# Second bias tile made in pieces under the first attention tile and parked in DRAM, with a new lead table for the first MoE

## The chip, the cores and the metric

One core of one Trainium2 chip runs the whole program. The metric is the device time of one execution in microseconds (us). Engines are named as in the profile: PE (TensorE), DVE (VectorE), ACT (ScalarE), POOL (GpSimd), and SP, whose queue issues all DMAs of this kernel.

## The reference, cut to what matters

Attention with a learned bias, then two MoE layers, in float32:

```python
x = (log1p(|i - j|) / log1p(max(i, 1)))[..., None]        # 576 x 576
bias = relu(x @ w1 + b1) @ w2                             # one 576 x 576 matrix for each of 8 heads
scores = q @ k.T / 8 + bias                               # 4 batches, 8 heads, 576 positions, depth 64
attn = softmax(scores); x = attn @ v                      # -> 2304 tokens of 512
x = (silu(x @ w_gate) * (x @ w_val)) @ w_out              # first MoE, hidden 1536
out = relu(x @ w_in) ** 2 @ w_out2                        # second MoE, hidden 2048
```

## The kernel before, in words

The 576 query positions are cut into four tiles of 128 (t = 0, 1, 2, 3) and a rest of 64, which is handled for two heads at once (t = "m"). For each tile `attend` walks over *items*, one item being one batch and one head: 32 items for each of the tiles 0 to 3 and 16 merged ones for the rest, 144 in all. An item is a score product on PE (`scores`, L813, four matmuls; L808 in the rest), the bias added and the row minimum taken on DVE (`soft`, L822), the exponential on ACT, a transpose of the result, and the product with v. In tile 0 the transpose is done on PE (L851) and the product with v is L865. In the later tiles the result is split in two float16 halves on POOL (L834, L220), transposed by a DMA (`pT<-pt`, issued on SP at L859), and multiplied by v in L875. In tile 1 `load_pair` and `split_pair` also fetch v again, split it, and store the split form in DRAM (`v_d`), beside loading k from DRAM (`kp<-kT_d`).

The bias matrix does not depend on the batch. `make_bias(t)` makes it for one tile and all eight heads before that tile's items use it. It works in 18 blocks of 32 key positions. Each block takes one mask on DVE (L605), 16 matmuls of 64 columns on PE (L644) into one PSUM bank, and an evacuation that turns the bank into 32 columns of the bias. The evacuation alternates between two forms: two instructions on DVE (L623, L629), or two on ACT (L620, L626) and two on POOL (L621, L627). The bias of a tile lies in one of two rooms of SBUF, `room0` and `room1`: tile 0 in room 1, tile 1 in room 0, tile 2 in room 1. While tile 0 is computed, room 0 also holds k and v of every second load and the results of tile 0 (`kvb` is room 0).

The first MoE (`moe1`) works in nine *units* of 256 tokens. Each attention tile makes two units ready, the rest makes the ninth. A unit has 288 matmuls for gate and value (L459, 24 for each of twelve blocks, each followed by tanh and products in `th` on ACT and DVE, L467 to L470, and a split in `z`, L444 and L220) and 72 for the output projection (L482). Its weights are decoded from 64-bit floats on DVE (`decode`, L262 to L267) and split by `w_stream`, which runs merged with tile 0.

All of this is written as Python generators that yield an estimated cost. `merge` mixes several of them by rates; `a_all` is the attention stream (tile 0 merged with the weights, then `rest`, which makes bias 1 by itself and then runs tiles 1 to 3 and "m", each merged with the next bias, and last `weights2`, which prepares the second MoE). `m_all` is the stream of the nine units. The outer loop steps the units' stream only when the attention stream is far enough ahead by a table:

```python
lead = base is not None and pos["a"] >= base + float(np.interp(pos["m"], *LEAD))
if m_ok and (lead or not a_ok):
    step("m", sm)
```

`pos` is the yielded cost of each stream, and one unit is 46.8 of it. A scheduler then fixes the order of instructions on each engine from this program order. Each engine and the SP queue work strictly in that order. After tile "m" and `weights2`, the second MoE (L1377, L1409) runs on PE to the end.

## Time and profile before

| | us |
|---|---|
| three runs of the kernel before | 1240.95, 1244.9, 1245.37 |
| their median | 1244.9 |
| the profiled execution's own time | 1241.07 |
| its span, from first to last instruction | 1238.9 |
| PE, DVE, ACT, POOL busy in that span | 1089.9, 778.1, 678.0, 651.8 |

A busy time is the union of the spans of an engine's instructions. A matmul's span is partly modelled and overlaps its neighbour's, so a PE that shows busy all through a stretch need not work at its peak. In the tables by stretch "(x91)" is the number of instructions, the column after the engines is the granted TensorE clock (1.00 is 2.4 GHz, 0.50 is 1.2 GHz, a value between is a mean over the stretch), and the last two are the mean busy share of the 16 DMA engines and what they moved.

### The profile page before, as it was taken

Reading aid. Unit: us, or ns where it says so; the run is one execution under the profiler, and the core shown is the slowest. Engines: PE = TensorE matmul, PEld = TensorE weight load, DVE = VectorE, ACT = ScalarE, POOL = GpSimd, SP = SyncE. Lnnn points to the kernel's source line nnn. Section 1 sums busy time; section 2 is a strip of 40 time slices with the busy share of each in tenths; the row PEclk is TensorE's granted clock in tenths of the full one; section 3 lists DMA queues with packets and bytes.
Section 4 is the critical chain, followed back from the end, with each engine's and each line's share of the span. In section 5 each row is a group of like instructions: output and inputs, shape, how many; then the busy total and the mean of one; then the engine's idle time right before and its main releaser. Section 6 shows DMA issues by size and latency. Waiting matters only on the chain.

```text
span 1238.9 us, 27332 instructions
## 1 busy us (share of the span) xinstructions
PE 1089.9 (88%) x10550; PEld 812.1 (66%) x10550; DVE 778.1 (63%) x1864; ACT 678.0 (55%) x1370; POOL 651.8 (53%) x835
## 2 busy tenths in 40 slices
PE   2577899998678889999997999979789999999998
PEld 2466788686467568686774767556348476584787
DVE  5988957887677667656665745895573442624423
ACT  3567767557566566566663543366462643616433
POOL 2433213269768687878784452237791532705423
PEclk9789799999979999999999999989999999999999
DMA  9957543219999998997989995660010010010100
GB/s 222 263 136 206 179 132 87 50 58 198 222 218 204 227 212 165 231 186 162 191 161 257 248 220 142 206 188 1 17 34 19 18 43 27 20 33 17 27 27 17
DMA packets 278078, 163.20 MB, mean 132 GB/s; under 512 B 233276, under 2 KB 246588, under 8 KB 277948
## 3 DMA queue, kind: packets, MB, share of 16 engines
q1 hardware_dynamic: 277948, 161.46, 55.0%
q8 instruction: 82, 1.34, 0.5%
q14 instruction: 48, 0.39, 0.1%
HBM read 92.13 MB, written 19.48 MB: 90 GB/s over the span
## 4 chain that ended last, share of the span: by engine, by line
PE 45%; DMA 14%; POOL 10%; DVE 8%; issue 5%; ACT 4%; SPq 2%; POOLq 0%; ACTq 0%; DVEq 0%
PE mm L1377 12%; PE mm L459 11%; PE mm L1409 10%; DMA pT<-pt 3%; PE mm L482 3%; POOL pt L220 3%; POOL x L1189 2%; PE ma L1409 2%; PE av L875 2%; PE qk L813 2%; DMA w2s<-in_moe_w_out_dram 2%; DMA qT<-qs 2%; DMA scrap<-in_moe_w_in_dram 1%; DMA kp<-kT_d 1%; DMA xT<-xh 1%
## 5 line engine op out<-in xcount | busy, mean ns | idle before, releaser
L459 PE MATMUL mm<-xT,wr 128*128 128x256 f16 x2400 | 288.7, 276 | 14.9 <-DVE th L470 7.3
L459 PEld LDWEIGHTS <-wr 128*128 128x128 f16 x2592 | 251.6, 99 | 53.2 <-issue 19.3
L1189 POOL TENSOR_TENSOR x<-x 128x256 f32<-128x256 f32 (+1 forms) x160 | 142.7, 903 | 178.1 <-ACT x L1386 171.7
L220 POOL TENSOR_TENSOR pt<-s,pt 128x512 f16<-128x512 f32 x224 | 172.1, 791 | 31.5 <-ACT pt L837 26.7
L220 POOL TENSOR_TENSOR z<-th,z 128x256 f16<-128x256 f32 x108 | 79.8, 740 | 129.5 <-ACT z L444 124.7
L482 PE MATMUL mm<-wr,z 128*128 128x512 f16 x612 | 142.3, 379 | 1.6 <-DVE sc L829 1.3
L822 DVE CUSTOM_DVE_ANT_0 s<-qk,room 128x576 f32<-128x576 f32 x144 | 107.7, 748 | 39.9 <-PE qk L813 22.6
L1409 PEld LDWEIGHTS <-wr 128*128 128x128 f16 x1134 | 110.6, 98 | 22.7 <-DVE wr L1189 4.3
L830 ACT ACTIVATE s<-s,sc 128x576 f32<-128x576 f32 x112 | 85.6, 772 | 56.6 <-DVE sc L829 47.1
L1189 DVE TENSOR_TENSOR wr<-x,wr 128x768 f16<-128x768 f32 (+3 forms) x60 | 75.4, 1268 | 64.5 <-ACT wr L1196 63.3
L1377 PE MATMUL mm<-wr,w2r 128*128 128x512 f16 (+1 forms) x480 | 102.2, 364 | 5.0 <-ACT x L1382 5.0
L482 PEld LDWEIGHTS <-z 128*128 128x128 f16 x648 | 60.0, 98 | 66.4 <-issue 2.8
L605 DVE TENSOR_TENSOR scrap<-scrap,room 128x1024 f16<-128x1024 f16 (+1 forms) x108 | 87.3, 822 | 22.4 <-PE ma L644 19.8
L1377 PE MATMUL mm<-wr,room 128*128 128x512 f16 (+1 forms) x480 | 100.1, 358 | 0.0
L621 POOL TENSOR_TENSOR scrap<-scrap 128x256 f32<-128x256 f32 (+1 forms) x90 | 63.2, 702 | 65.9 <-ACT scrap L620 58.2
L875 PE MATMUL av<-vp,pT 128*128 128x65 f16 (+3 forms) x1792 | 70.4, 196 | 28.3 <-DMA pT<-pt 24.3
L875 PEld LDWEIGHTS <-pT 128*128 128x128 f16 (+1 forms) x1792 | 61.7, 102 | 43.2 <-DMA pT<-pt 32.7
L1377 PEld LDWEIGHTS <-w2r 128*128 128x128 f16 x480 | 47.6, 99 | 52.7 <-issue 8.6
L644 PEld LDWEIGHTS <-scrap 128*128 128x128 f16 x1440 | 59.6, 104 | 27.4 <-issue 11.9
L1377 PEld LDWEIGHTS <-room 128*128 128x128 f16 x480 | 46.9, 98 | 45.6
L1428 ACT ACTIVATE ob<-ob,fac 128x256 f32<-128x256 f32 x36 | 17.8, 506 | 105.5 <-DVE ob L1427 105.5
L444 ACT CAST z<-th 128x256 f16<-128x256 f32 x108 | 42.8, 399 | 59.0 <-DVE th L470 57.8
(289 smaller groups left out, 2157.2 us busy)
## 6 DMA issues: line engine op xcount, KB each, us to landing
kp<-kT_d SPq DMA_DIRECT2D x64, 288.0 KB, 3.5
vp<-v_d SPq DMA_DIRECT2D x48, 325.0 KB, 3.5
w2s<-in_moe_w_out_dram SPq DMA_DIRECT2D x16, 512.0 KB, 4.0
wr<-in_moe_w_gate_dram SPq DMA_DIRECT2D x24, 256.0 KB, 5.2
wst<-in_moe_w_out_dram SPq DMA_DIRECT2D x12, 512.0 KB, 4.0
wr<-in_moe_w_val_dram SPq DMA_DIRECT2D x24, 256.0 KB, 4.2
v_d<-vp SPq DMA_DIRECT2D x16, 325.0 KB, 3.1
y_d<-yh SPq DMA_DIRECT2D x18, 256.0 KB, 3.5
```

Of the source, the lines that this page charges most:

```text
L220: nc.gpsimd.tensor_tensor(out=out_, in0=x, in1=hi, op=ALU.subtract)
L459: nc.tensor.matmul(pg[:, 256 * gi:256 * gi + 256], wr.parts(key, f // 4, cc, wl, P * (f % 4), P), mov(xl, cc), start=k == 0, stop=k == 11)
L482: nc.tensor.matmul(po, zall[:, f, zl, P * t:P * t + P], wr.parts("o", 0, f, wl), start=k == 0, stop=k == 3 * NF1 - 1)
L605: nc.vector.tensor_tensor(out=m[:, :, ni * e:ni * e + ni], in0=block(kb, i0, ni), in1=th, op=ALU.is_gt)
L621: nc.gpsimd.tensor_tensor(out=tmp[r], in0=tmp[r], in1=xb, op=ALU.mult)
L644: nc.tensor.matmul(pv[:, :, :, c:c + 4], m[:, a, :], bd[:, l], start=l == 0, stop=l == 1)
L822: nc.vector.tensor_tensor_reduce(out=s.rearrange("p (a j) -> p a j", a=2), in0=pq[:, :, 0:288], in1=bias[:, n].rearrange("p (a j) -> p a j ...
L830: nc.scalar.activation(s, s, AF.Exp, bias=nm, scale=-1.0)
L875: nc.tensor.matmul(av[r, slot, 0:cn], pT[:, 5 * l + c, r], vs[e][c][:, c0:c0 + cn], start=m == 0, stop=m == 13)
L1189: (nc.gpsimd if how else nc.vector).tensor_tensor(out=out_, in0=a, in1=b, op=op)
L1377: nc.tensor.matmul(ph[:, :n], w2r.parts("w", g // 4, cc, wl, P * (g % 4), P), yt[:, 4 * yl + cc, :], start=m == 0, stop=m == 11)
L1409: nc.tensor.matmul(po, HS[f][:, o:o + P], st["C7"][f][wl][:, b:b + 256], start=f == 0 and k == 0, stop=f == 7 and k == 2)
```

## The change: what it does

`make_bias(1)` no longer stands alone ahead of tile 1. It is a third generator merged with tile 0 and the weight stream. Each of its 18 blocks waits until a given number of tile 0's items are done (`("av", 8 + kb)`), makes its mask only then, takes its PSUM bank from the two `mm` banks that the weight stream and the units use (before: from the score banks), and is evacuated into one of two small buffers (`bst`), from where a DMA stores it in DRAM (`b_d`). At the start of `rest`, `fetch_bias` reads the 18 blocks back into room 0 with three DMAs. The addition in `soft` reads them through a four-dimensional view for tile 1. The lead table gets other numbers: less of the units at first, more from the end of the second unit on.

```diff
-LEAD = [0, 39, 78, 117, 260, 400], [0, 85.669, 132.183, 165.544, 287.094, 406.094]
+LEAD = [0, 28, 93.6, 327, 400], [0, 82.0, 127.0, 333.0, 389.0]
...
+    b_d = dram.tile([P, 18, 256], F32, name="b_d")
...
-        merged = t == "m"
+        merged, afar = t == "m", t == 1
...
-        bias = rooms[{0: 1, 1: 0, 2: 1, 3: 0, "m": 1}[t]]
+        bias = rooms[0 if t == 3 else 1]
...
+                to = bst[:, kb % 2] if afar else bias[r, :, cs]
...
                     nc.vector.scalar_tensor_tensor(
-                        out=bias[r, :, cs], in0=pv[r, 1, hs], scalar=st["kB"][r], in1=tmp[r],
+                        out=to, in0=pv[r, 1, hs], scalar=st["kB"][r], in1=tmp[r],
                         op0=ALU.mult, op1=ALU.add)
+                if afar:
+                    nc.sync.dma_start(b_d[:, kb, :], to.rearrange("p h j -> p (h j)"))
...
-            if kb + 1 < nb:
+            if kb + 1 < nb and not afar:
                 mask(kb + 1)
+            if afar:
+                yield ("av", 8 + kb)
+                mask(kb)
             m = masks.pop(kb)
-            pv = ma().rearrange("p (z h j) -> p z h j", z=2, h=8)
+            pv = (mm if afar else ma)().rearrange("p (z h j) -> p z h j", z=2, h=8)
...
+    def fetch_bias():
+
+        room = rooms[0][:, 0:8 * S].rearrange("p (k x) -> p k x", k=18)
+        for k0, k1 in ((9, 13), (0, 9), (13, 18)):
+            nc.sync.dma_start(room[:, k0:k1], b_d[:, k0:k1])
+        st["bias", 1] = room.rearrange("p k (h j) -> p h k j", h=8)
...
+    bst = pre.tile([P, 2, 8, 32], F32, name="bst")
...
+        fetch_bias()
         scale_v(ma)
-        early[0] = True
-        yield from make_bias(1)
-        early[0] = False
...
-        yield from merge((sa, 25.5), (w_stream(), 70.0))
+        yield from merge((sa, 25.5), (w_stream(), 70.0), (make_bias(1), 30.0))
```

The order of instructions shows it at three places. Line numbers of the changed kernel are higher: L844 there is the softmax addition that is L822 before, L607 the mask L605, L626 and L632 the two DVE evacuations L623 and L629, L666 the fetch.

The first place is DVE in the second half of tile 0, at the additions of the items with index 18 and 19 (`ISA s`). Before, the stretch ahead of an addition holds weight decoding (`wr<-wst`) and splitting:

```order
L265 SCALAR_TENSOR_TENSOR wr_97<-wst_128,wr_97 128x512
L904 TENSOR_REDUCE sc_1615<-sc_1308 128x1
L751 COPY qs_1764<-qs_1764 128x4x64
L267 SCALAR_TENSOR_TENSOR wr_97<-wst_128,wr_97 128x512 x2
L191 SCALAR_TENSOR_TENSOR wr_97<-wr_97,keep11_1255 128x512
L822 ISA s_1698,sc_1699<-qk_1687,room1_115 128x576
L822 ISA sc_1699 128x1
```

With the change:

```order
L844 ISA s_1872,sc_1873<-qk_1777,room1_116 128x576
L844 ISA sc_1873 128x1
L760 SCALAR_TENSOR_TENSOR qs_2007<-qf_2005,qs_2007 128x4x64
L626 SCALAR_TENSOR_TENSOR scrap_117<-mm_1602,keep4_216,scrap_117 128x256
L607 TENSOR_TENSOR scrap_117<-scrap_117,room1_116 128x1024
L192 SCALAR_TENSOR_TENSOR wr_98<-wr_98,keep11_1260 128x512
L844 ISA s_1920,sc_1921<-qk_1886,room1_116 128x576
L844 ISA sc_1921 128x1
```

An evacuation and a mask of bias 1 now stand between two additions of tile 0. In the whole order 12 of the 18 masks stand ahead of tile 0's last addition, 3 of them in its first sixteen items.

The second place is DVE at the first additions of tile 1, which read room 0. Before, masks and evacuations of the biases alternate with the `th` products of the second unit:

```order
L468 SCALAR_TENSOR_TENSOR th_3932<-th_3932,mm_3905 128x256
L629 SCALAR_TENSOR_TENSOR room0_114<-qk0_3185,keep4_214,scrap_116 128x8x32
L605 TENSOR_TENSOR scrap_116<-scrap_116,room1_115 128x1024
L470 SCALAR_TENSOR_TENSOR th_3932<-th_3932,mm_3905 128x256
L822 ISA s_3277,sc_3278<-qk_3244,room0_114 128x576
L822 ISA sc_3278 128x1
```

With the change:

```order
L192 SCALAR_TENSOR_TENSOR vp_3120<-junk1_114,keep25_3106,vp_3120 64x2x64
L469 SCALAR_TENSOR_TENSOR th_3194<-th_3194,mm_3167 128x256
L471 SCALAR_TENSOR_TENSOR th_3194<-th_3194,mm_3167 128x256
L192 SCALAR_TENSOR_TENSOR wr_98<-wr_98,keep23_2661 128x512
L607 TENSOR_TENSOR scrap_117<-scrap_117,room1_116 128x1024
L844 ISA s_3198,sc_3199<-qk_3140,room0_115 128x576
L844 ISA sc_3199 128x1
```

The `th` products here are still those of the first unit. On PE, 336 matmuls of L459, 72 of L482 and 288 of L644 stand between the last score of tile 0 and the first of tile 1 before; with the change 186, none and 112. By the items with index 56 to 64 the two orders have issued the same unit matmuls again to within a few blocks.

The third place is the SP queue ahead of tile 1's first loads of k (`kp`). Before:

```order
L739 DMA qf_3853<-in_q_dram 128x4x64
L765 DMA kp_3222<-kT_d0_63 128x1152
L765 DMA kp_3237<-kT_d0_63 128x1152
L925 DMA_TRANSPOSE xT_2706<-xh_2707 128x8x128
L925 DMA_TRANSPOSE xT_2706<-xh_2711 128x8x128
L776 DMA junk1_113<-in_v_dram 64x2x64
```

With the change:

```order
L600 DMA scrap_117<-in_c_x_dram 128x576
L636 DMA b_d_71<-bst_130 128x256 x2
L946 DMA_TRANSPOSE xT_3076<-xh_3081 128x8x128
L666 DMA room0_115<-b_d_71 128x1280
L781 DMA kp_3118<-kT_d0_63 128x1152
L781 DMA kp_3133<-kT_d0_63 128x1152
```

The two loads of k stood ahead of the second unit's transposes (`xT`); they now stand behind them and behind the last stores and the last fetch of bias 1.

## Rows read from the trace of the kernel before

**Rows 1.** Engine busy time by stage: the eleven stretches of this study, all engines

```profile
core 0: us, PE busy (x) PEld busy (x) DVE busy (x) ACT busy (x) POOL busy (x), PEclk, DMA share, GB/s
67.40:130.60 63.20, 50.02 (x432) 41.39 (x430) 55.43 (x130) 46.04 (x88) 18.68 (x15) 0.94 0.68 173
130.60:197.20 66.60, 57.00 (x484) 50.88 (x482) 46.81 (x134) 51.51 (x111) 14.96 (x13) 0.87 0.48 146
197.20:270.60 73.40, 69.61 (x765) 55.90 (x763) 58.24 (x148) 40.51 (x90) 31.80 (x39) 1.00 0.21 58
270.60:303.40 32.80, 30.23 (x393) 25.01 (x393) 25.47 (x68) 24.65 (x54) 29.84 (x40) 1.00 0.76 164
303.40:361.80 58.40, 42.02 (x481) 28.92 (x480) 40.19 (x109) 34.76 (x78) 44.40 (x63) 0.80 1.00 221
361.80:402.80 41.00, 35.59 (x445) 30.54 (x444) 31.24 (x79) 28.32 (x65) 32.11 (x48) 1.00 0.95 206
402.80:456.50 53.70, 46.16 (x539) 32.40 (x539) 35.31 (x105) 31.48 (x62) 38.66 (x53) 0.97 1.03 222
456.50:519.60 63.10, 63.08 (x766) 49.48 (x765) 42.73 (x127) 38.70 (x81) 52.51 (x73) 1.00 0.93 191
519.60:743.00 223.40, 202.61 (x2492) 154.13 (x2490) 137.72 (x432) 127.01 (x277) 150.46 (x234) 0.98 0.95 206
743.00:930.00 187.00, 162.32 (x1167) 103.36 (x1166) 129.41 (x268) 98.69 (x200) 98.78 (x95) 0.96 0.34 97
930.00:1238.90 308.90, 302.83 (x2206) 215.19 (x2204) 122.84 (x152) 127.61 (x218) 113.20 (x132) 1.00 0.09 25
```

**Rows 2.** Line L813, score matmuls of tiles 1 to 3

```profile
L813 PE MATMUL qk<-kp,qT x384: 282/286/448, 270.6 to 658.4; 128*128 128x288 f16 x192
```

**Rows 3.** Groups of instructions, 235 to 272 us, lines of make_bias

```profile
L605 DVE TENSOR_TENSOR scrap<-scrap,room 128x1024 f16<-128x1024 f16 x18 | 15.1, 842 | 1.2 <-PE qk L644 1.1
L644 PE MATMUL qk<-bd,scrap 128*128 128x64 f16 x288 | 10.4, 193 | 1.8 <-ACT room L626 1.4 <-DVE sc L150 0.4
L621 POOL TENSOR_TENSOR scrap<-scrap 128x256 f32<-128x256 f32 x9 | 8.5, 940 | 14.5 <-ACT scrap L620 14.5
L627 POOL TENSOR_TENSOR room<-room,scrap 128x256 f32<-128x256 f32 x9 | 8.6, 951 | 0.7
L620 ACT ACTIVATE scrap<-qk,keep 128x256 f32<-128x256 f32 x9 | 4.2, 467 | 0.5 <-PE qk L644 0.2
L623 DVE SCALAR_TENSOR_TENSOR scrap<-qk,keep,scrap 128x256 f32<-128x256 f32 x9 | 4.2, 472 | 0.0
L629 DVE SCALAR_TENSOR_TENSOR room<-qk,keep,scrap 128x256 f32<-128x256 f32 x8 | 3.8, 472 | 0.0
```

**Rows 4.** Line L605 (a mask) in 235 to 272 us: shortest, median and longest

```profile
L605 DVE TENSOR_TENSOR scrap<-scrap,room x18: 675/697/1219, 236.4 to 271.2; 128x1024 f16<-128x1024 f16 x18
```

**Rows 5.** Chain of waits: 24 matmuls of L459, then 12 of L482

```profile
256.83 2.62 PE mm L459 x24
493.96 2.59 PE mm L482 x12
```

**Rows 6.** DMA queues and issues, 271 to 450 us: KB each, median us to landing

```profile
q1 hardware_dynamic: 87090, 36.97, 95.6%
kp<-kT_d SPq DMA_DIRECT2D x22, 288.0 KB, 3.5
y_d<-yh SPq DMA_DIRECT2D x3, 256.0 KB, 3.6
```

**Rows 7.** Waits in 271 to 450 us: total us, times, longest

```profile
PEld L875 <- DMA pT<-pt: 20.3, 19, 3.6
PE av L875 <- DMA pT<-pt: 15.7, 17, 3.5
```

**Rows 8.** Timeline of PE, 343 to 362 us: start, us, instruction [idle before]

```profile
354.83 4.33 PE L459 MATMUL mm<-xT,wr 128*128 128x256 f16 x22 [0.92 <-DMA xT<-xh]
360.29 0.60 PE L875 MATMUL av<-vp,pT 128*128 128x65 f16 x14 [0.69 <-DMA pT<-pt]
```

More of the change, by code (lines that the diff above doesn't have):

```diff
@@ L595, in make_bias @@
         bias = bias[:, 0:nh * S].rearrange("p (h j) -> p h j", h=nh)
-        st["bias", t] = bias
+        if not afar:
+            st["bias", t] = bias
         xs = scrap[:, 1536:1536 + S]
@@ L821, in soft @@
         nm = scr([P, 1], tag="nmx")
+        sv, qv, bv = s.rearrange("p (a j) -> p a j", a=2), pq[:, :, 0:288], bias[:, n]
+        if len(bias.shape) == 4:
+            sv, qv = [x.rearrange("p a (k j) -> p a k j", j=32) for x in (sv, qv)]
+            bv = bv.rearrange("p (a k) j -> p a k j", a=2)
+        else:
+            bv = bv.rearrange("p (a j) -> p a j", a=2)
         nc.vector.tensor_tensor_reduce(
-            out=s.rearrange("p (a j) -> p a j", a=2), in0=pq[:, :, 0:288],
-            in1=bias[:, n].rearrange("p (a j) -> p a j", a=2), op0=ALU.add, op1=ALU.min,
+            out=sv, in0=qv, in1=bv, op0=ALU.add, op1=ALU.min,
             accum_out=nm, scale=-1.0 / C, scalar=1e30)
```

7 lines of the change are left out of this document (4 added, 3 removed).

## The prediction

> **What bounds the kernel now.** Read first the busy time by stage [rows 1]. Its first nine limits are starts of score matmuls: 67.4, 130.6 and 197.2 us are the first, the seventeenth and the last item of tile 0, 270.6 is the first item of tile 1 [rows 2], 402.8 the first of tile 2, 519.6 the last but one of tile 2; 743 and 930 enclose the second MoE's weights. The reader is to see who is full in each line. In tile 0 DVE is busy 55.4 of 63.2 us and then 46.8 of 66.6, and the DMA engines are at 0.68 and 0.48. In the *transition* (197.2 to 270.6), where the kernel before makes bias 1, PE is busy 69.6 of 73.4 us, but not with attention: it runs the first unit, half of the second, and the bias blocks, while the DMA engines stand at 0.21. From 303.4 to 743 it is the other way round: the DMA share is 0.93 to 1.03, and PE has idle time of 16.4, 5.4 and 7.5 us in the three stages from 303.4 to 456.5. The DMA queue view confirms it, 95.6% of all 16 engines [rows 6]; there PE waits 20.3 and 15.7 us for transposes [rows 7]. After 930 PE is full, and nothing of the change lies there. So the bubble is one of DMA, not of PE: the transition is full of PE work, and the stage behind it is short of it.
>
> **What the change does to each engine.** Work is moved, hardly any is added. The order of instructions tells how much.
>
> *Tile 0 gets 12 of the 18 blocks.* On DVE that is 12 masks of 0.842 us and, for every second block, two evacuations of 0.472 us [rows 3]: 12 x 0.842 + 6 x 2 x 0.472 = 15.8 us. PE gets 192 matmuls at 10.4 / 288 = 0.036 us [rows 3], 6.9 us. ACT (0.467 us an instruction) and POOL (0.940 and 0.951) get two for each of the other six blocks [rows 3], 5.6 and 11.3 us; POOL is busy 18.7 and 15.0 us in the two halves, so it has room. DVE has 7.8 us idle in the first half and 19.8 in the second [rows 1]. The price lies between 0 (all of it fits the idle time) and 15.8 us (all of it delays the softmax). Three blocks fall in the fuller half and nine in the looser one, and DVE and ACT work in one chain with PE; I take 9, a little over the middle.
>
> *The transition loses PE work.* 150 matmuls of L459 at 2.62 / 24 = 0.109 us are 16.4 us, 72 of L482 at 2.59 / 12 = 0.216 us are 15.5 us [rows 5], and 176 bias matmuls are 6.3 us: 38.2 us. If PE stayed as full as it is, 73.4 would become 35.2. What is late next is the SP queue: the last fetch waits for the landing of the last stores, and the first two loads of k stand behind it. A store and a load of such size bracket this: 256 KB land in 3.6 us and 288 KB in 3.5 [rows 6], some 7 us after the last evacuation; the order has 66 matmuls of L459 (7.2 us) between the last bias-1 block and the first score of tile 1, which cover most of it. I add 3 us and take 38.4, that is 35 less. Ends: 40 less (PE gaps close too) and 26 less (7 us of landing uncovered and a wait of 2 more). The 18 stores and 3 fetches move 4.7 MB, where the queue is idle for half or more of the time: nothing, unless they fall behind 270.
>
> *The stages behind get the 31.9 us of unit work back*, since by the items with index 56 to 64 the orders are level. In their order (item index in brackets):
> - 270.6 to 303.4 (32 to 41): PE gets 5.8 us more where 2.6 are idle: +5.
> - 303.4 to 361.8 (42 to 53): PE gets 18 us more. Idle are 16.4, and in this stage the granted clock averages 0.80 [rows 1]: 22 matmuls take 4.33 us behind a wait for a transpose [rows 8], against 2.62 for 24 elsewhere [rows 5]. With the clock kept at 1.00, PE's 42.0 us would need about 8 less and all would fit. But the DMA share of 1.00 lets nothing get shorter: +3.
> - 361.8 to 402.8 (54 to 63): 3 us more (bias 2 comes later), 5.4 idle: +2.
> - 402.8 to 519.6 (64 to 93): 19 us more, then 15 less. PE would have 113.5 of 116.8 us, the DMA engines 114 (1.03 x 53.7 + 0.93 x 63.1): between -2 and +8, since the two can't be full at every moment; +5.
> - Behind 519.6 the orders and the sums agree: 0.
>
> Together +15, with ends of 0 (all in idle time) and +26 (the idle time is waits that order and landings make, and can't be filled).
>
> *Small edits.* The four-dimensional view in `soft` adds the same 576 elements. No row shows it so; if it cost 0.1 us on 32 items, 3 us of DVE in tile 1, where DVE is idle a quarter of the time [rows 1]: nothing.
>
> **The sum**: 9 - 35 + 15 = -11 us. The profiled execution took 1241.07 us, 3.8 below the median of its three runs (1244.9) and at their low end. That makes 1230 beside the profile and 1234 beside the median; I put 1232.
>
> **The rivals.**
>
> *Given back.* The two idle sums are almost equal: PE has 2.6 + 16.4 + 5.4 + 7.5 = 31.9 us idle from 270.6 to 456.5, and 31.9 us are moved there. For it: PE takes its instructions in order, and the waits of rows 7 come with that order; more unit work between two items does not make the transposes land earlier. Against it: 303.4 to 361.8 holds half of the idle time, and there PE ran long gaps at half clock. If only 6 of the 31.9 us fit, the stages cost +26: 9 - 35 + 26 = 0, 1241. Chance 0.20.
>
> *Slower, by the two `mm` banks.* A weight column's norm keeps one of the two banks while four chunks are decoded; unit blocks and bias blocks then take turns in the other. If a block's mask, matmuls and evacuation all come in series with the softmax, it costs 0.842 + 16 x 0.036 + 2 x 0.472 = 2.4 us [rows 3], 28.8 for twelve in place of 9: -11 + 20 = +9, 1250. It decides from about 17 us on: when the last score of tile 0 starts after 214, the gain is under 0.5%, and after 223 it is a loss. For it: before, these blocks used the score banks and found them free. Against it: the later part of the weight stream (`second`) takes a bank only at its end. Chance 0.13.
>
> *DVE and POOL at one port.* In the rows the masks are 0.675 us at the shortest, 0.697 at the median, 0.842 at the mean and 1.219 at the longest [rows 3, 4]: some are stretched while POOL works on the same bias. If each of the 12 POOL instructions of tile 0's blocks stopped DVE for its whole 0.94 us, that is 11.3 us, of which 12 x (0.842 - 0.675) = 2.0 is in the mean already: +9 on DVE, in all -2, 1239. The Trainium skill, page SBUF — State Buffer, section "Who interferes with whom", states the rule: a DVE instruction with two SBUF inputs and a GpSimd instruction that reads SBUF exclude each other for the whole instruction, and whichever issues second waits. By that rule the sum would be nearer to -2 than to -11. The spread of the masks agrees with it, but half of them run within 0.03 us of the shortest although POOL's 18 instructions fill 17.1 us of the same 37 [rows 3], so I leave it a rival: chance 0.09.
>
> *More gain.* If the unit work in 303.4 to 361.8 keeps the clock at 1.00 and the DMA engines stay as full as before, the stages cost +3 in place of +15: -23, 1218. Against it speaks that 402.8 to 519.6 has 3 us to spare on PE and on DMA alike. Chance 0.12.
>
> That the change does not do what it says is excluded by the order: the masks, the stores and the later units are where the diff puts them.
>
> **How the numbers follow.** The forecast keeps 0.46, with its own range of 1222 to 1240. A difference of 0.5%, 6 us, is about what a measurement of this kernel tells from no change. Faster by more: most of the forecast (0.40), the larger gain (0.12), and a little of the port and of the work given back (0.03): 0.55. Within: the rest of those three, 0.29. Slower: the banks (0.13) and the tail of the work given back (0.03): 0.16. The range for 8 in 10 reaches from just under the larger gain, 1216, to just under the loss by the banks, 1248.
>
> **What would show it.** Right: the first score of tile 1 starts between 240 and 250 us in place of 270.6; the last score of tile 0 near 206; the transition has some 38 us; DMA is at 0.9 or more from 280 on; PE in the stage of items 42 to 53 is 50 us busy or more, its clock above 0.80; the first item of tile 2 starts 15 to 18 us earlier than before, and tile "m" ends some 11 earlier. Wrong: the last score of tile 0 after 214 (banks or port; the longest wait would then be of DVE or PE for an `mm` bank, or masks longer than 0.84); the first addition of tile 1 waiting over 5 us for the fetch; the stages of tile 1 longer by 20 us or more at a lower DMA share (the work given back).

## The result, and the profile after

The changed kernel takes 1254.33 us (median of 9 runs, 1248.90 to 1257.49), the kernel before 1245.77 (9 runs beside them): their medians are 8.6 us apart, where 1232 was forecast. The ratio of the means is 1.0058 [1.0034, 1.0083] (in brackets the 95% interval), so it is slower by more than the noise. The profiled execution of after took 1255.24 us, that of before 1241.07, so the two traces differ by 14.6 us of span, 6 more than the medians do.

The busy time by stage in the kernel after, with the same marks as [rows 1]: first, seventeenth and last item of tile 0, then the first items of index 32, 42, 54, 64, 80, 94 and 143. Columns as there: length, busy us of each engine, granted clock, DMA share.

```profile
core 0: us, PE busy (x) PEld busy (x) DVE busy (x) ACT busy (x) POOL busy (x), PEclk, DMA share, GB/s
67.50:133.70 66.20, 55.17 (x484) 45.01 (x482) 59.62 (x145) 46.47 (x89) 22.48 (x18) 0.87 0.64 165
133.70:212.50 78.80, 62.80 (x626) 55.17 (x624) 59.50 (x145) 57.05 (x122) 20.56 (x22) 0.87 0.49 140
212.50:260.60 48.10, 37.80 (x367) 31.86 (x365) 35.07 (x97) 25.66 (x57) 17.22 (x23) 0.86 0.42 122
260.60:303.10 42.50, 37.36 (x393) 25.43 (x394) 28.52 (x80) 28.20 (x61) 31.72 (x44) 0.96 0.92 193
303.10:361.10 58.00, 53.84 (x572) 40.75 (x572) 34.09 (x105) 34.59 (x78) 36.34 (x53) 0.97 0.84 175
361.10:410.80 49.70, 39.78 (x499) 33.50 (x498) 36.91 (x96) 32.55 (x76) 37.19 (x53) 0.97 0.85 198
410.80:477.50 66.70, 62.62 (x764) 48.25 (x764) 41.29 (x125) 39.14 (x81) 52.35 (x71) 1.00 1.00 198
477.50:530.90 53.40, 49.38 (x602) 36.35 (x600) 34.64 (x104) 31.51 (x64) 39.76 (x55) 1.00 1.00 196
530.90:754.00 223.10, 202.37 (x2474) 153.82 (x2471) 145.72 (x428) 127.49 (x277) 156.44 (x238) 0.97 0.96 207
```

Three things stand in these rows. Tile 0 takes 145.0 us where it took 129.8. The transition, 212.5 to 260.6, takes 48.1 in place of 73.4, but PE is busy 37.80 of it, 79%, where it was 69.61 of 73.4, 95%. And the stages from item 32 to 94 take 270.3 us in place of 249.0, with PE busy 80 to 94% of each. The first score of tile 1 (line L829, L813 in [rows 2]) does come 10 us earlier:

```profile
L829 PE MATMUL qk<-kp,qT x384: 283/286/448, 260.6 to 671.9; 128*128 128x288 f16 x192
```

**An account of PE's time** says more than the stages. Each stretch is split in three: PE idle (length less busy), lost at half clock (half of the busy time under a granted clock of 0.50), and the rest, which is PE's work at full clock. Before and after, from the two traces, us:

| stretch | length | work at full clock | idle | lost at half clock |
|---|---|---|---|---|
| tile 0 (items 0 to 31) | 129.8, 145.0 | 95.3, 101.7 | 22.8, 27.0 | 11.8, 16.3 |
| transition (to item 32) | 73.4, 48.1 | 69.6, 32.4 | 3.8, 10.3 | 0.0, 5.4 |
| items 32 to 94 | 249.0, 270.3 | 207.5, 238.0 | 31.8, 27.3 | 9.6, 5.0 |
| all the rest | 786.7, 790.1 | 681.5, 682.1 | 90.6, 90.3 | 14.5, 17.6 |
| whole span | 1238.9, 1253.5 | 1053.9, 1054.2 | 149.0, 154.9 | 35.9, 44.3 |

The work is the same to 0.3 us. 37.2 us of it left the transition, and 6.4 + 30.5 = 36.9 came back elsewhere at full price. What the change could win or lose lies in the last two columns alone: items 32 to 94 gave up 9.1 us of them, while tile 0 and the transition took on 20.6.

What a stretch at half clock looks like is seen at 162.7 to 179.8, in tile 0's preparation of k and v. Windows, then the timeline of PE there (start, us, instruction, idle before it and what ended it):

```profile
150.00:162.70 12.70, 9.14 (x99) 7.90 (x98) 12.66 (x35) 9.21 (x23) 2.61 (x3) 1.00 0.56 150
162.70:179.80 17.10, 14.77 (x79) 12.63 (x78) 5.27 (x17) 8.76 (x17) 1.26 (x1) 0.50 0.42 130
179.80:192.00 12.20, 10.81 (x151) 9.87 (x150) 10.47 (x22) 8.46 (x16) 2.90 (x3) 1.00 0.52 138
```

```profile
162.19 0.69 PE L872 MATMUL tr<-ident,s 128*128 128x128 f32 x4 [1.39 <-ACT s L848]
...
168.97 1.01 PE L722 MATMUL ma<-ident_h,room 128*128 128x128 f16 x8 [1.65 <-ACT kva L724]
169.78 6.61 PE L886 MATMUL av<-room,pT 128*128 128x64 f32 x30
...
176.78 4.22 PE L460 MATMUL mm<-xT,wr 128*128 128x256 f16 x24
```

In the 12.7 us ahead, DVE is full (12.66) and PE idle for 3.6. Then the granted clock is 0.50 for 17.1 us; 24 matmuls of the unit take 4.22 us, against 2.79 at full clock further down, and DVE is busy 5.27 of 17.1. The rest of that time DVE waits for POOL (4.6 us), for ACT (5.9) and only 1.3 us directly for PE.

### The profile page after: what moved, and what is told of

It is laid out like the page before. It is cut to its first block, busy times and chain, and to the rows that moved or that the text cites. A ratio compares the mean times of both kernels' runs of the same rounds, so it can differ in the third digit from the quotient of the medians.

```text
span 1253.5 us, 27381 instructions
## 1 busy us (share of the span) xinstructions
PE 1098.4 (88%) x10550; PEld 815.4 (65%) x10550; DVE 779.2 (62%) x1864; ACT 678.1 (54%) x1370; POOL 653.1 (52%) x835
## 4 chain that ended last, share of the span: by engine, by line
PE 41%; DMA 21%; DVE 16%; POOL 9%; ACT 5%; issue 5%; SPq 2%; POOLq 0%; ACTq 0%; DVEq 0%
PE mm L1397 12%; PE mm L1429 10%; PE mm L460 8%; DMA pT<-pt 6%; PE mm L483 3%; DMA qT<-qs 3%; POOL pt L221 2%; DMA w2s<-in_moe_w_out_dram 2%; POOL x L1209 2%; DVE scrap L607 2%; PE ma L1429 2%; DVE s L844 2%; DMA wr<-in_v_dram 2%; PE av L896 2%; DMA wst<-in_moe_w_out_dram 2%
## 5 line engine op out<-in xcount | busy, mean ns | idle before, releaser
L460 PE MATMUL mm<-xT,wr 128*128 128x256 f16 x2400 | 296.6, 281 | 19.0 <-DVE th L471 9.7
L483 PE MATMUL mm<-wr,z 128*128 128x512 f16 x612 | 145.6, 385 | 0.9 <-POOL z L221 0.7
L844 DVE CUSTOM_DVE_ANT_0 s<-qk,room 128x576 f32<-128x576 f32 x112 | 83.9, 750 | 33.5 <-PE qk L829 21.7
L607 DVE TENSOR_TENSOR scrap<-scrap,room 128x1024 f16<-128x1024 f16 (+1 forms) x108 | 87.4, 822 | 15.2 <-PE ma L653 13.1
L653 PEld LDWEIGHTS <-scrap 128*128 128x128 f16 x1440 | 59.5, 105 | 27.4 <-issue 13.7
L829 PE MATMUL qk<-kp,qT 128*128 128x288 f16 x384 | 64.5, 288 | 7.9 <-DMA kp<-kT_d 5.5
```

Of the source, the lines that this page charges most:

```text
L460: nc.tensor.matmul(pg[:, 256 * gi:256 * gi + 256], wr.parts(key, f // 4, cc, wl, P * (f % 4), P), mov(xl, cc), start=k == 0, stop=k == 11)
L483: nc.tensor.matmul(po, zall[:, f, zl, P * t:P * t + P], wr.parts("o", 0, f, wl), start=k == 0, stop=k == 3 * NF1 - 1)
L607: nc.vector.tensor_tensor(out=m[:, :, ni * e:ni * e + ni], in0=block(kb, i0, ni), in1=th, op=ALU.is_gt)
L829: nc.tensor.matmul(pq[:, j, 0:288], qT[:, 2 * (n % 4) + s, :], kts[0][:, js], start=s == 0, stop=s == 1)
L844: nc.vector.tensor_tensor_reduce(out=sv, in0=qv, in1=bv, op0=ALU.add, op1=ALU.min, accum_out=nm, scale=-1.0 / C, scalar=1e30)
```

## The experiments

Eighteen kernels ran. The table gives, beside each kernel's time and its ratio to the kernel before, four starts (last item of tile 0, items 32, 64 and 94), and the idle and half-clock sums of its trace as above. The ratio is that of the means, to runs of the kernel before made beside that kernel, so it isn't the quotient of the medians in the table. e7, e8, e10, e19 and e20 leave part of the function out. Where a kernel orders the unit work otherwise, the starts compare only with that in mind.

| kernel | us | ratio | item 31 | 32 | 64 | 94 | idle | half |
|---|---|---|---|---|---|---|---|---|
| before | 1245.8 | 1 | 197 | 271 | 403 | 520 | 149 | 36 |
| after | 1254.3 | 1.0058 [1.0034, 1.0083] | 213 | 261 | 411 | 531 | 155 | 44 |
| e1_old_lead | 1269.5 | 1.0172 [1.0117, 1.0227] | 209 | 271 | 405 | 527 | 157 | 48 |
| e2_new_lead | 1251.4 | 1.0042 [1.0010, 1.0074] | 199 | 270 | 408 | 539 | 147 | 45 |
| e3_store_act | 1245.9 | 0.9992 [0.9963, 1.0021] | 213 | 266 | 404 | 524 | 153 | 35 |
| e4_bank_ma | 1251.3 | 1.0028 [0.9998, 1.0058] | 239 | 252 | 411 | 532 | 152 | 49 |
| e5_actpool | 1253.6 | 1.0043 [1.0024, 1.0061] | 213 | 259 | 408 | 528 | 154 | 41 |
| e6_dve | 1255.5 | 1.0062 [1.0037, 1.0087] | 208 | 262 | 412 | 533 | 154 | 43 |
| e7_fewmask | 1246.7 | 0.9991 [0.9967, 1.0015] | 213 | 260 | 405 | 524 | 147 | 49 |
| e8_no_fetch | 1253.3 | 1.0053 [1.0027, 1.0080] | 212 | 257 | 406 | 526 | 151 | 38 |
| e10_no_blocks | 1232.5 | 0.9892 [0.9859, 0.9924] | 206 | 214 | 373 | 499 | 143 | 49 |
| e11_gate_early | 1262.3 | 1.0124 [1.0091, 1.0157] | 220 | 240 | 402 | 526 | 155 | 51 |
| e12_gate_late | 1257.6 | 1.0081 [1.0046, 1.0115] | 194 | 270 | 416 | 551 | 153 | 50 |
| e13_late_act | 1266.8 | 1.0160 [1.0100, 1.0220] | 196 | 275 | 422 | 561 | 164 | 53 |
| e14_depth3 | 1264.0 | 1.0136 [1.0099, 1.0174] | 213 | 261 | 402 | 528 | 159 | 50 |
| e15_before_depth3 | 1246.4 | 0.9987 [0.9972, 1.0002] | 200 | 273 | 411 | 525 | 148 | 49 |
| e17_pT_act | 1341.8 | 1.0747 [1.0705, 1.0788] | 211 | 259 | 423 | 566 | 212 | 62 |
| e18_z_dve | 1255.2 | 1.0073 [1.0047, 1.0098] | 214 | 265 | 414 | 532 | 152 | 47 |
| e19_after_no_kv | 1245.0 | 0.9997 [0.9971, 1.0023] | 210 | 258 | 403 | 519 | 146 | 38 |
| e20_before_no_kv | 1240.5 | 0.9952 [0.9922, 0.9981] | 199 | 272 | 390 | 516 | 146 | 46 |

### Which part: the lead table or the move

e1_old_lead is the kernel after with the lead table of before, e2_new_lead the kernel before with the new table.

```diff
-LEAD = [0, 28, 93.6, 327, 400], [0, 82.0, 127.0, 333.0, 389.0]
+LEAD = [0, 39, 78, 117, 260, 400], [0, 85.669, 132.183, 165.544, 287.094, 406.094]
```

> The changed kernel with the lead table of before; the bias pieces stay as changed. Lead theory (the new table moves too much unit work behind tile 1's first item, where it is paid again): tile 0 as in the changed kernel (last score near 212 us), but the stages from tile 1 on pay less; 8 to 15 us faster than the changed kernel, 1240 to 1246. Chain theory (the bias work in tile 0 is paid in full there, and where the units stand matters little because PE is full anyway): within 4 us of the changed kernel, 1250 to 1257.

> The kernel before with the new lead table; bias 1 stands alone as before. Its order has 384 gate and value matmuls and 72 of the output projection ahead of tile 1's first score (432 and 72 before, 282 and 0 in the changed kernel). Lead theory: slower than before by 4 to 10 us. Chain theory: the table alone is worth little, within 4 us of before.

By the ratios the move alone costs 1.7% (about 21 us), the table alone 0.4% (5) and the two together 0.6% (7). e2's time fits the lead theory at its low end; that of e1 was missed by both theories: with the old table the transition holds 12 us more of work and idles no less, 12.3 of 62.7 us, so tile 0's loss stands against hardly any gain. The table softens the move; it isn't the main cause of the loss.

### Tile 0: what the twelve blocks cost

Five edits of after change one thing each in how the blocks of bias 1 are made: the queue of the stores (e3), the PSUM bank (e4), the evacuation all on ACT and POOL (e5) or all on DVE (e6), and 16 of the 18 masks left out (e7).

```diff
-                    nc.sync.dma_start(b_d[:, kb, :], to.rearrange("p h j -> p (h j)"))
+                    nc.scalar.dma_start(b_d[:, kb, :], to.rearrange("p h j -> p (h j)"))
...
-            pv = (mm if afar else ma)().rearrange("p (z h j) -> p z h j", z=2, h=8)
+            pv = ma().rearrange("p (z h j) -> p z h j", z=2, h=8)
...
-                how = mixed("b" if t in (0, 1) else "B")
+                how = 2 if afar else mixed("b" if t in (0, 1) else "B")
...
-                how = mixed("b" if t in (0, 1) else "B")
+                how = 0 if afar else mixed("b" if t in (0, 1) else "B")
...
-                mask(kb)
-            m = masks.pop(kb)
+                if kb < 2:
+                    mask(kb)
+            m = masks[kb % 2] if afar else masks.pop(kb)
```

> The changed kernel with the 18 stores issued on ACT's queue in place of SP's; the three fetches stay on SP. Queue theory (a store that waits on SP for an evacuation holds up the loads of weights and of tile 0's data behind it, which makes the tile and the transition longer): the last score of tile 0 comes 5 to 10 us earlier than the 212.5 us of the changed kernel, the waits of DVE decode for the output projection's weights go, 1242 to 1247. Chain theory: last score of tile 0 within 3 us of 212.5, time within 4 us of the changed kernel; it may even lose 1 to 2 us of ACT time for issuing.

> The changed kernel with the bias blocks in the single ma bank, as the later tiles have it, and not in the two mm banks shared with the weight stream and the units. Bank theory (blocks and unit work wait for each other's bank): last score of tile 0 by 204 us or earlier, 1243 to 1248. Chain theory: no earlier than 209, time within 4 us of the changed kernel.

> The changed kernel with all 18 blocks of bias 1 evacuated by ACT and POOL, none by DVE. That takes 9 x 2 x 0.472 = 8.5 us off DVE (6 us of it in tile 0) and puts 8.4 on ACT and 17 on POOL. DVE theory (tile 0 is as long as DVE's work in it): last score 5 to 6 us earlier than 212.5, the time 5 us below the changed kernel. Port theory (POOL's bias work holds DVE up): last score later by 4 us or more, masks longer than 0.85 us, the time 4 us or more above the changed kernel. Latency theory (a block makes a round over DVE, PE and the evacuating engines inside the softmax's own round, and how long its instructions are matters little): last score within 3 us.

> The changed kernel with all 18 blocks evacuated by DVE, none by ACT and POOL: 8.5 us more on DVE, POOL without bias 1. DVE theory: last score 5 to 6 us later than 212.5. Port theory: masks near 0.69 us, last score 3 us or more earlier. Latency theory: within 3 us; the time within 4 us of the changed kernel.

> The changed kernel without 16 of the 18 masks of bias 1 (every block multiplies one of the first two masks; the bias of tile 1 is left out to that extent). 16 x 0.84 = 13.5 us less on DVE, ten of them in tile 0. DVE theory: last score 8 us earlier than 212.5, the time 8 us or more below the changed kernel. Latency theory: last score 3 us earlier at most, the time within 5 us.

The last score of tile 0 stays at 208 to 213 whether DVE makes all evacuations, none, or hardly a mask. The 208 is that of e6, all on DVE, and 24 fewer unit matmuls (2.6 us) stand ahead of it there. So the blocks' work on DVE, on which the forecast priced them, is by itself not what they cost there. It isn't the queue of the stores either (213 with e3). With the other bank (e4) all the blocks and 192 unit matmuls come ahead of that score, and it moves to 239 with the total nearly unchanged. The 8 us that e3 and e7 gained against after lie behind item 42, which starts at 307.7 and 303.4 us (after: 303.1), while item 94 starts at 523.8 and 523.9 (530.9). In e3 the half-clock sum is 9 us smaller. In e7 PE idles 6.1 us less in tile 0 than in after, but loses 8.0 us more there at half clock, so the masks that are left out do not show in the length of the tile.

Then the blocks were taken out, and moved. e10_no_blocks makes and fetches no bias 1; e11 and e12 gate each block seven items earlier or later; e13 is e12 with the stores on ACT's queue.

```diff
-        yield from merge((sa, 25.5), (w_stream(), 70.0), (make_bias(1), 30.0))
+        yield from merge((sa, 25.5), (w_stream(), 70.0))
...
-                yield ("av", 8 + kb)
+                yield ("av", 1 + kb)
...
-                yield ("av", 8 + kb)
+                yield ("av", 15 + kb)
```

> The kernel after without any block of bias 1 and without its fetch (the bias of tile 1 is left out: 288 matmuls, 18 masks, 36 evacuations, 18 stores, 3 fetches are not done; that is 10.4 us of PE work). Theory 1, work and waits (the blocks cost their PE time in full where they are put and make PE wait besides; the transition is a chain of small steps, norms, weight splits and landings, that PE idles under): the last item of tile 0 starts at 195 to 201 us as in the kernel before, in place of 213; the transition, which then holds hardly any unit work (48 matmuls of L459's kind against 186), still takes 28 us or more, with PE idle and at half clock for over 12 us together; the whole takes 1228 to 1240. Rival 1, the clock alone (versions differ by how much half-clock time they happen to meet, wherever the blocks are): tile 0 still ends past 207, and the total stays at 1241 to 1254. Rival 2, the transition is made of work: without blocks and units it takes under 20 us.

> All 18 blocks come seven items earlier, so all of them lie ahead of the last score of tile 0 and only 72 unit matmuls stand between it and the first score of tile 1. Theory 1 (work and waits): tile 0 gets longer by the six further blocks, last score at 217 to 225; the transition takes 28 to 38 us although it holds only 8 us of unit work; the first score of tile 1 comes at 250 to 258; the unit work left out of the transition is paid in items 32 to 64 in full; total within 6 us of the kernel after (1248 to 1260). Rival 1 (clock alone): total follows the half-clock time of its run. Rival 2 (the transition is work): first score of tile 1 at 235 to 242, total 1238 to 1246.

> The blocks come seven items later: 5 in place of 12 ahead of the last score of tile 0, and 240 bias matmuls with 216 and 43 unit matmuls in the transition. Theory 1 (work and waits): last score at 200 to 206, transition 54 to 62 us with PE less idle (under 8 us idle, since blocks and units fill the chain), first score of tile 1 at 257 to 264, and a total of 1244 to 1251, nearer to the kernel before. Rival 1 (clock alone): no less idle time than the kernel after, 1249 to 1258. Rival 3 (the two mm banks hold up whichever stage has the blocks): the transition takes 66 us or more, total over 1255.

> The later gates with the stores on ACT's queue: the two edits that stand best against their causes. Theory 1 (work and waits): as the later gates, and 4 to 8 us less as with the stores on ACT's queue alone: 1238 to 1246, which would be no slower than the kernel before. Rival 1 (clock alone; the 8 us gained by the stores on ACT's queue were clock): 1246 to 1255, about the same as the later gates alone.

The stages of e10, without blocks, and of e11, with all 18 in tile 0: items 0 to 15, items 16 to 30, and the transition.

```profile
69.30:134.50 65.20, 53.79 (x435) 43.49 (x433) 57.76 (x144) 45.54 (x86) 20.89 (x17) 0.87 0.65 175
134.50:206.40 71.90, 63.09 (x541) 55.87 (x539) 48.28 (x133) 56.17 (x120) 16.49 (x16) 0.91 0.45 136
206.40:214.20 7.80, 5.16 (x39) 4.12 (x37) 6.18 (x19) 5.74 (x13) 2.74 (x5) 0.85 0.43 110
```

```profile
66.40:132.60 66.20, 54.17 (x528) 45.05 (x526) 60.15 (x140) 47.63 (x92) 24.05 (x20) 0.91 0.70 177
132.60:220.00 87.40, 71.82 (x676) 62.58 (x674) 64.69 (x161) 58.47 (x124) 30.42 (x27) 0.80 0.44 133
220.00:240.30 20.30, 19.54 (x131) 17.00 (x131) 11.16 (x35) 9.79 (x22) 5.57 (x9) 0.75 0.28 75
```

Tile 0 takes 137.1 us in e10, but with 144 unit matmuls ahead of its last score where before, after and e11 have 96; 48 at 2.62 / 24 us each [rows 5] are 5.2, which leaves 131.9, near the 129.8 of before. So the blocks do it: 12 cost 15.2 us in after, 18 cost 153.6 - 129.8 = 23.8 in e11, about 1.3 us a block, of which a block's 16 matmuls are 0.58 [rows 3] and the rest is idle time and half clock. That is a mean and no constant: the 5 blocks that e12 and e13 leave in tile 0 cost about nothing there (126.1 and 128.0 us, with 24 fewer unit matmuls, 2.6 us).

Two things of my expectations failed. The transition without blocks takes 7.8 us, not 28, and e11's takes 20.3, of which only 0.7 are idle: here the rival was right that takes the transition for work, though e11's total of 1262.3 us fits neither theory. The norms of the weight stream, which I took for a chain that PE must sit through, come behind the first score of tile 1 in both kernels (up to 242.6 and 261.0 us), and PE waits for none of them there. So the idle time goes with the blocks that stand in the transition. And e12, with 5 blocks in tile 0 (last score at 194), gives back in the transition more than it wins: 76.0 us, of which 16.8 are idle and 10.0 lost at half clock, though 49.2 us of work stand there. The longest of PE's waits in it (193.8 to 269.7 us):

```profile
PE mm L653 <- DVE th L471: 6.0, 4, 3.1
PE mm L653 <- ACT bst L629: 3.1, 3, 1.5
PE mm L653 <- DVE bst L632: 2.4, 1, 2.4
```

With three shorter ones of the same kind they make 13.7 of the 16.8 us. These matmuls read neither `th` nor `bst`; what the evacuations set free for them is an `mm` bank. So the rival of the two banks, with its 66 us or more for the transition and over 1255 in all, came true for e12. In after such waits are 0.3 us in tile 0 and 2.8 in the transition. No run gates the blocks late and gives them another bank.

e10 also bounds the whole idea, roughly. It takes 1247.7 - 1232.5 = 15.2 us less than the runs of before on the same chip, and 10.4 of these are the matmuls of bias 1 [rows 3]. As an estimate, no place for the blocks could have gained more than about 5 with the new lead table; e10 has that table, which by itself cost 5 us in e2, so with another table the bound may be higher.

e13 shows how little an edit's effect carries over: the stores on ACT's queue took 8 us off after and put 9 on e12, and e13's 1266.8 us lie outside both of its theories.

### The transition: not the fetch

e8_no_fetch leaves the three fetches out, and with them the bias of tile 1.

```diff
-        for k0, k1 in ((9, 13), (0, 9), (13, 18)):
-            nc.sync.dma_start(room[:, k0:k1], b_d[:, k0:k1])
```

> The changed kernel without the three fetches: tile 1 adds what lies in room 0, so that its bias is left out; blocks and stores stay. Fetch theory (the transition of 48 us in place of the 38 I forecast is the last stores, the last fetch and the loads of k behind them on SP): first score of tile 1 at 250 to 254 in place of 260.6, 5 us or more off the time. Chain theory (the transition is DVE's, ACT's and PE's own chain of weight splits, unit products and norms): first score within 3 us of 260.

The first score comes 3.5 us earlier, between the two theories, and the total is that of after within 1 us. The transition takes 45.2 us in place of 48.1: the landing costs 2.9 us, as forecast (3). What the rest is shows the timeline of PE in the kernel after:

```profile
228.89 8.06 PE L460 MATMUL mm<-xT,wr 128*128 128x256 f16 x48 [1.90 <-DVE bst L632]
...
238.76 0.38 PE L170 MATMUL mm<-sc,ones_r 1*128 1x2 f32 x2 [1.58 <-DVE sc L167]
239.07 2.79 PE L460 MATMUL mm<-xT,wr 128*128 128x256 f16 x24
...
245.83 0.20 PE L698 MATMUL ma<-sc,ones_f 128*1 128x8 f32 x2 [3.19 <-DVE ux L930]
246.13 2.10 PE L653 MATMUL mm<-bd,scrap 128*128 128x64 f16 x32
...
260.64 1.14 PE L829 MATMUL qk<-kp,qT 128*128 128x288 f16 x8 [2.35 <-DMA junk<-in_v_dram]
```

Four waits of 1.6 to 3.2 us: for an evacuation, for two norms of tiny instructions (L167, L930), for a load of v. And 48 unit matmuls take 8.06 us, at half clock for most of it, against 2 x 2.79 = 5.6. In the kernel before, bias blocks and more unit work stood in this stage, and PE idled for 3.8 us in all.

### Items 32 to 94: how far the moved work was hidden

PE's waits there (261 to 531 us) in the kernel after: total us, times, longest.

```profile
PE av L896 <- DMA pT<-pt: 15.3, 17, 2.1
PE qk L829 <- DMA kp<-kT_d: 5.5, 3, 3.8
```

In the kernel before, items 32 to 94 have 15.7 us in 17 waits for transposes, all of them those of [rows 7]: in sum, 30 us more of unit work took next to nothing off them. By stage it looks otherwise. The waits in items 42 to 53, before and after:

```profile
PE av L875 <- DMA pT<-pt: 7.5, 7, 3.5
PE av L896 <- DMA pT<-pt: 0.6, 2, 0.4
```

There 17.9 us more of work at full clock took no more time (58.4 us before, 58.0 after): idle time and half clock together fell from 24.3 to 5.9. The waits for transposes grew in the other stages, from 2.2 to 4.5 us in items 32 to 41, from 2.2 to 2.9 in 54 to 63 and from 3.7 to 7.3 in 64 to 93, and idle time and half clock together rose by 4.3 and 6.1 us in the first two and fell by 1.1 in the third. So the moved work was hidden where it fell on idle time, and more than half of what that won (10.4 of 18.4 us) was lost in the stages beside it.

Ahead of a transpose the SP queue itself waits, mostly for POOL (SP's waits, the same stretch):

```profile
SPq L880 <- POOL scrap L624: 17.2, 9, 2.5
SPq L880 <- POOL z L221: 16.3, 10, 2.7
SPq L880 <- POOL room L630: 13.1, 12, 2.0
```

The line with `z` is the units' own work on POOL, and more of it stands here than before (9.5 us there). Four runs gave the transposes more time, or took work away ahead of them: one more item between scores and product, in after (e14) and in before (e15); the transposes issued from ACT's queue (e17); the low half of z on DVE (e18).

```diff
-            if len(pend_av) == 2:
+            if len(pend_av) == (2 if t == 0 else 3):
...
-        nc.sync.dma_start_transpose(out=pT[:, 0:9, :], in_=pt.rearrange("p l j -> p (l j)"))
+        nc.scalar.dma_start_transpose(out=pT[:, 0:9, :], in_=pt.rearrange("p l j -> p (l j)"))
...
-                rest_of(zall[:, f, 1, :], th, zall[:, f, 0, :])
+                nc.vector.tensor_tensor(out=zall[:, f, 1, :], in0=th, in1=zall[:, f, 0, :], op=ALU.subtract)
```

> The kernel after, with one more item between an item's scores and its product with v in tiles 1 to m (three products pending in place of two; the same number of buffers). Theory T (the moved unit work filled no idle time because PE, in order, comes to the product with v before the transpose has landed, 15 us in items 32 to 94 before and after alike): the wait of the products with v for transposes falls from 15.3 us to under 7, items 32 to 94 get 6 to 10 us shorter, total 1242 to 1248. Rival D (the DMA engines are the bound there, share 0.85 to 1.00, and a transpose that is waited for less is only replaced by another load that is waited for): the wait changes place, for kp or for qT, and the stages keep their 270 us within 4; total 1250 to 1258.

> The kernel before with the same edit. Theory T: the waits for transposes (15.7 us) fall by more than half, items 32 to 94 take 240 us or less in place of 249, total 1236 to 1242, which would beat both kernels. Rival D: the same stages within 4 us of before, total 1244 to 1250.

> The kernel after, with the transposes of tiles 1 to m issued from ACT's queue in place of SP's. SP's queue waits for POOL ahead of a transpose (splits of the softmax, of z and of the bias) and holds the loads behind it meanwhile. Rival Q (the order of SP's queue makes transposes and loads late): the wait for kp falls (5.5 us) and the one for transposes too, total 1244 to 1250. Theory T (the time from the softmax to the landing is what counts, and ACT then waits for POOL in its own order): ACT's exponentials come later, the products with v wait as long or longer, total 1255 to 1270.

> The kernel after, with the low half of a unit's z made on DVE (rest of its split) in place of POOL. In items 32 to 94 POOL stands 13.8 us waiting for ACT's half of z, with the splits of the softmax queued behind it, and SP waits 16.3 us for that z ahead of transposes (9.5 in the kernel before, which has fewer unit blocks there). Theory P (the moved unit work brings its own wait: its z on POOL makes the transposes late): waits for transposes fall from 15.3 to under 9 us, items 32 to 94 take 258 to 264 us in place of 270, total 1242 to 1249. Rival D (DMA engines): stages within 4 us, total 1250 to 1258. Rival V (DVE becomes the chain: 38 x 0.67 us more ahead of additions): waits for DVE grow, total over 1258.

PE's waits for transposes from 261 to 531 us, in e14, in e15 and in e18:

```profile
PE av L896 <- DMA pT<-pt: 6.9, 4, 4.1
```

```profile
PE av L875 <- DMA pT<-pt: 21.7, 23, 3.8
```

```profile
PE av L896 <- DMA pT<-pt: 9.9, 11, 3.3
PE qk L829 <- DMA kp<-kT_d: 8.4, 4, 3.2
```

In e14 and e18 the wait fell by 8.4 and 5.4 us and the stages by 3.6 and 3.1 (266.7 and 267.2 us): in e18 another wait, for kp, grew by 2.9, and in e14 the half-clock loss from 5.0 to 9.1. In e15 it did not even fall, and the stages took 251.6 us (before: 249.0). Neither version beats the kernel before; e14 is even slower than after, since it takes 5.6 us more in items 94 to 143 and 5.7 more behind them. e17 is a plain loss: from 261 to 531 us SP's own transposes (L773, L946) wait 62.7 us, up to 8.1 at a time, for the landing of those on ACT's queue, and PE idles 212 us in the whole run.

That left the DMA engines, the bound that the forecast had named. e19 and e20, of after and of before, load no k and v from tile 2 on: those tiles compute with the last two pairs that tile 1 loaded.

```diff
     def load_pair(b, a, strm, raw=None):
 
+        if raw is None:
+            kp, vp = kept[-1 - a % 2]
+            hold["k", b, a] = kp
+            for i in range(2):
+                hold["v", b, 2 * a + i] = [vp[:, i, c] for c in range(5)]
+            return
```

> The kernel after, in which tiles 2, 3 and m use the last two pairs of k and v that tile 1 loaded and load none themselves (so their scores and products use the k and v of other batches; some 18% of the bytes of items 64 to 94 are not moved). Theory D (behind item 54 the DMA engines are the bound, at a share of 0.85 to 1.10, which is why a wait removed in the last runs came back as another): items 64 to 94 take 112 to 116 us in place of 120.1 (PE's work at full clock there is 112.0), items 94 to 143 take 197 to 209 in place of 222.7 (195.2), total 1228 to 1240. Theory T (the bound is the time of each transpose after the softmax, in the order of POOL and SP; the share of the DMA engines only looks full): items 94 to 143 keep 216 us or more, PE waits for transposes as long as before, total 1246 to 1254.

> The kernel before with the same loads left out. Theory D: items 64 to 94 take 110 to 114 us in place of 116.8 (PE's work 107.5), items 94 to 143 take 199 to 211 in place of 221.7 (197.8), total 1222 to 1234, and the kernel after stays some 6 to 8 us behind, since what it lost lies ahead of item 64. Theory T: total 1238 to 1246.

Items 80 to 93, 94 to 127 and 128 to 142 of e19:

```profile
470.00:519.30 49.30, 48.69 (x597) 36.14 (x596) 33.12 (x103) 30.64 (x62) 39.55 (x54) 1.00 0.67 121
519.30:667.60 148.30, 133.81 (x1578) 103.87 (x1574) 94.41 (x286) 90.98 (x205) 116.42 (x186) 0.98 0.66 119
667.60:739.30 71.70, 67.56 (x893) 50.60 (x892) 47.63 (x144) 37.62 (x73) 41.34 (x53) 0.95 0.74 130
```

From item 94 to 143, 27 MB are moved in place of 46 (GB/s by length) and the DMA share falls from 0.96 to 0.69, yet the stretch takes 220.0 us in place of 222.7. Items 64 to 93 take 116.2 in place of 120.1. In e20 items 94 to 143 take 223.7 (before: 221.7). So a DMA share of 0.9 to 1.0 was no bound there: with two fifths of the bytes gone, the time of these items stays. The Trainium skill, page Perfetto Trace Analysis, section "Identifying the Most-Contended Engine", says to judge DMA by HBM utilization and not by occupancy, "since 16 DMA engines make occupancy misleading"; these two runs agree that it misleads.

The loads are not free for all that. e20 is 6 us faster than before (0.9952 [0.9922, 0.9981]), within theory T's range, and e19 by the ratios about as much faster than after (0.9997 and 1.0058), between the ranges of the two theories. In the traces items 32 to 94 are shorter, 260.9 us in e19 (after: 270.3) and 244.0 in e20 (before: 249.0). In e20 tile 2 starts 12.5 us earlier, so its items 64 to 93 hold 9.6 us more work and take 125.5 us in place of 116.8.

No version that computes the whole function beats the kernel before by more than its interval; e3 (0.9992) and e15 (0.9987) equal it.

## Why the prediction was wrong

**The bound.** "The bubble is one of DMA, not of PE" is the sentence that failed first; it took the busy share of the DMA engines for a limit. e19 and e20 show that they do not bound the items from 94 on, whatever their share, and items 64 to 93 of the kernel after hardly (116.2 us at a share of 0.68, 120.1 at 1.00). For items 32 to 64 no run takes bytes away, and the question stays open there: e1 and e2 took 45.9 us for items 42 to 53 in place of 58.4, but moved only 9.4 and 9.6 MB there in place of 12.9 (GB/s by length; e1, then e2):

```profile
309.10:354.90 45.80, 42.84 (x443) 32.22 (x440) 30.58 (x91) 28.49 (x67) 28.75 (x44) 0.96 0.93 206
304.80:350.80 46.00, 36.97 (x379) 23.13 (x378) 30.48 (x91) 27.88 (x63) 32.09 (x46) 0.91 0.92 208
```

PE's work at full clock is the fixed part (1048 to 1058 us in every kernel that does all the work). That its idle time comes from the time that one item takes through DVE, ACT, POOL, SP and a transpose is argued from the waits and not shown.

**Tile 0, +9 taken, +15.2 in the traces.** The mechanism was priced on the wrong engine. DVE's 15.8 us were counted, and PE's 6.9 us of matmuls named but left out of the sum. e5, e6 and e7 show that less or more of DVE's part does not change the tile's length, e10 and e11 that a block costs 1.3 us there in the mean, matmuls, idle time and half clock together. The three traces with tile 0 as before have 129.8, 133.5 (e15) and 130.6 us (e20), the six with tile 0 as in after (after, e8, e14, e17, e18, e19) 143.1 to 146.1, so by the medians about 14 of the 15 repeat.

**The transition, -35 taken, -25.3 in the trace.** The work was counted well: 38.2 us were to go and 37.2 went; the landing was taken at 3 and cost 2.9. What failed, with the largest miss of the three, is "if PE stayed as full as it is". It stayed at 79%, not 95: 10.3 us idle and 5.4 at half clock. The idle time came with the blocks of bias 1 that still stood there: without any, PE idled 2.6 us (e10), 0.7 (e11) and 0.3 (e4), with 13 of them 16.8 (e12) and 19.8 (e13). That the work taken away had covered the small waits of after is possible, but not shown; e12 idled more with more work in the stage.

**Items 32 to 94, +15 taken, +21.3 in the trace.** 31.9 us of work were to come back, and 30.5 did, stage by stage about as counted (5.4, 17.9, 2.7 and 4.5; the 113.5 us of PE work forecast for items 64 to 93 are 113.2 by its own rows). In items 42 to 53 the room was there, as the forecast said: +3 was taken and -0.4 came, at a clock of 0.97, while the DMA share fell to 0.84, where it was to be what "lets nothing get shorter". The step that failed is the price of the other stages: +5, +2 and +5 were taken, and +9.7, +8.7 and +3.3 came, since new idle time and half clock opened in items 32 to 41 and 54 to 63. So some 17 us were to go into idle time, and in sum idle time and half clock fell by 9.1. The ends of this term, 0 and +26, held it. The rival "given back" had the sum of the waits right (15.7 and 15.3 us for transposes), but not their places, and it left the other two terms at +9 and -35, and so came to 0. All three terms missed to the same side, by 6, 10 and 6 us, and the stages from item 94 on, taken at 0, with the start of the program took 3.4 more. With before's own profile 4.7 us under its median and after's 0.9 over, 8.6 us remain between the medians.

**The other rivals.** *The two `mm` banks* had the sign, and the last score at 212.5 was near its mark of 214; but in tile 0, where it put the cost, PE waits only 0.3 us for such a bank, and with the other bank (e4) the total is 1251.3, its interval overlapping that of after. So the cause there is another; in the transition the banks have a part, 2.8 of the 10.3 idle us in after. *DVE and POOL at one port*: with every evacuation on ACT and POOL or every one on DVE the times are 1253.6 and 1255.5, with overlapping intervals, and the twelve masks in tile 0 have a median of 0.692 us in after, 0.764 in e5, 0.680 in e6. The order of these three agrees with the Trainium skill (page SBUF — State Buffer, section "Who interferes with whom"), by which a DVE instruction with two SBUF inputs contends with a GpSimd instruction that reads SBUF; the time does not hang on it. *More gain* had items 42 to 53 right and not the stages beside them.

**The small edits** showed no price: the additions in tile 1 (L844, four-dimensional view) have a median of 0.751 us from 261 to 300 us, against 0.745 in the kernel before.

**Open** stays what would fill the idle time, and why new idle time opened in items 32 to 41 and 54 to 63. Over the kernels that do all the work, e17 aside, the idle sum is 147 to 164 us wherever the blocks, stores, splits or waits are put; which link of an item's chain sets it no run here isolates. Open too is why the same edit took 8 us off (e3) or added 9 (e13); the half-clock sums (35 and 53 us) go along with it, but were not varied by themselves.

## What to carry to other kernels

Before moving work off a full engine, split each stage into work, idle time and time at half clock: the work is paid wherever it goes, so a move is worth only the idle time and half clock that it removes less those that it opens elsewhere, and a stage where PE is 95% busy has little to win. Idle time in one stage can be real room, as in items 42 to 53 here, and the move still lose by what opens in the stages beside it: price these too. A busy share of the DMA engines near 1 is tested by taking bytes away, not by reading it. And price a step on every in-order engine that it passes, the matmuls on PE first.

## What was not expected of the hardware

The mean share of the DMA engines told of no limit: 0.96 and 0.69 go with 222.7 and 220.0 us for the same items. The transposes issued from ACT's queue instead of SP's took the kernel after from 1254.3 to 1341.8 us (1.0747 [1.0705, 1.0788] of before), by far the largest effect of any edit. And 17.1 us at half clock stood behind a stretch of 12.7 us in which PE was idle for no more than 3.6.
